# Idle matmuls between attention and the first expert, and the last logits from f16 pairs

## The chip, the core and the metric

The kernel runs on one core of a Trainium2 chip. A time is the device time of one execution in microseconds. The engines of the core run beside each other and wait for one another through semaphores: TensorE (PE; its weight loads are shown as PEld), VectorE (DVE), ScalarE (ACT), GpSimd (POOL) and SyncE (SP, which only issues DMAs). PE runs at one of two clock levels, 1.2 or 2.4 GHz; the profile shows the granted share of the higher one, 0.50 or 1.00.

## The reference

Bucketed attention over 4 batches of 8 heads (768 positions, head size 64), then a mixture of 8 experts in which tokens and experts are matched greedily, highest logit first, with room for 384 tokens at each expert:

```
mask = q_bucket[:, :, :, None] == k_bucket[:, :, None, :]      # buckets: signs of q @ proj, k @ proj
scores = np.where(mask, scale * np.matmul(q, k.transpose(0, 1, 3, 2)), -1e9)
attn = np.exp(scores - max); attn = attn / (sum + 1e-09); x = attn @ v   # heads side by side: 3072 x 512
logits = x @ w_gate                                             # 3072 x 8
for idx in np.argsort(-logits.flatten()):
    tok, e = idx // E, idx % E
    if assigned[tok] >= 0 or counts[e] >= cap: continue
    assigned[tok] = e; counts[e] += 1
out[mask_e] = np.maximum(x[mask_e] @ w1[e], 0.0) @ w2[e]        # for every expert e
```

## The kernel before

**Attention** goes head by head (32 of them, `NH`), in slots: scores on PE (L240, L258, L259), exponents on ACT (L260), the values' matmul on PE (L273 to L275, closed by six small ones at L279), the division on DVE (`norm`, L287 to L290). Products of full precision are made of f16 or bf16 pairs, a high part and what is left of it. After every second head the 128 new columns of x (a tile `X`) are transposed on PE against an identity matrix (`xtr`, L309), split on ACT (L310) and DVE (L311) into an f16 pair `XH`, `XL`, and multiplied by the gate's weights, which are a pair too (`logits`, L318 and L319). The very last 128 columns, those of heads 30 and 31, go another way (`xlast`, `flast`): the transposed tile stays f32 (copied by ACT for one half and by DVE for the other, L301), and six f32 matmuls (L304) add their share to the logits; DVE then sums the two parts into `Lm` (L305).

**Routing of expert 0** (`Moe.early` and `Moe.phase(0)`) follows on the critical path. It looks for the threshold logit at which the first expert is full: the logits' bits are cut into six digits; for each digit DVE compares all tokens with a table (`compare`, L530), PE counts (`count`, L540 once and L541 24 times, with 8 moving columns each), DVE finds the digit (L635), one matmul carries it to all partitions (L642), and DVE forms the next comparand (L649). The first digit's table has 128 columns, the others' 32. Then come the ties (L660 and the DVE chain behind it), running sums (L687, L688), the list of the expert's tokens (`members` on DVE, `collect` on PE, L699), and POOL issues three indirect DMAs that gather their rows of x (`gather`, L763). `xsplit0` transposes the three gathered tiles (L827, four f32 matmuls each) and splits them (L828, L829); then expert 0's first layer begins (`layer1c`, L843).

Between these steps PE already runs a few idle matmuls, `warm` (L576, L577): 128 columns, with a result that nobody reads. Their numbers stand in the table `KW`: after each count (`KW[0]`), after the digit's matmul (`KW[1]`), behind L660 (`KW[2]`), behind L688 (`KW[3]`), behind each of the three blocks of `collect` (`KW[4]`), behind L748 (`KW[5]`), between the transposes (`KW[6]`), and once behind the first count (`KW[7]`).

The order on every engine is the order in which the program is written (a manual schedule): an idle matmul stands in PE's queue before what is written after it, and what is written after it waits until it is through. The kernel's later experts are one long row of matmuls on PE (L858, L870), with the routing of the next expert between them.

Of the kernel before, what the change touches and what calls it, by code (L numbers as in the profile page):

```python
# [8 lines left out]
F32 = mybir.dt.float32  # L9
# [6 lines left out]
AX = mybir.AxisListType  # L16
# [3 lines left out]
AP=dict(PAT=[[5], [3]],  # L20
 E0=[3, 5],
 E1=[3, 4],
 X=[2, 2, 5],
 MR=2,
 LEAD=9,
 S=[7, 7],
 DW=[12, 0, 0, 0, 384],
 P1=[13, 13, 14, 16, 17, 17, 23, 21, 16, 27, 21, 26, 23, 24, 33, 32, 3, 4, 49, -7, 3, 13],
# [17 lines left out]
def attention(tc, nc, ctx, qT, kT, vv, proj, wg, x_dram, L, jp, identf, B, late=None, after=None):  # L46
# [234 lines left out]
    X={}  # L281
# [12 lines left out]
    XH,XL=(XT[:,2*i:2*i+2].bitcast(F16).rearrange("p d c q -> p (d c q)").rearrange("p (d c q) -> p d c q",d=4,c=6) for i in range(2))  # L294
    def wsplit():
        A.copy(wgs[:,:,0],wgr); G_.tensor_tensor(wgs[:,:,1],wgr,wgs[:,:,0],op=ALU.subtract)
    def xlast(b,d,hf):
        ps=psT.tile([128,512],F32,name="pst"); p=ps[:,0:384].rearrange("p (c q) -> p c q",c=3); r=slice(3*hf,3*hf+3)
        for c in range(3):
            T.transpose(p[:,c],X[b][:,3*hf+c,d*128:d*128+128],identf)  # L300
        (V.tensor_copy if hf else A.copy)(XT[:,1,r],p)  # L301
    def flast(b,d):
        p=LP[-1][:,0:96].rearrange("p (c z e) -> p c z e",c=6,z=2)
        for c in range(6): T.matmul(p[:,c,0],XT[:,1,c],wgr[:,d],start=False,stop=c==5,skip_group_check=True)  # L304
        V.reduce_sum(L[:,b*6:b*6+6],p.rearrange("p c z e -> p c e z"),axis=AX.X)  # L305
    def xtr(b,d,hf):
        ps=psT.tile([128,512],F32,name="pst"); p=ps[:,0:384].rearrange("p (c q) -> p c q",c=3); r=slice(3*hf,3*hf+3)
        for c in range(3):
# [3 lines left out]
    LP=[]  # L312
    def logits(b,ds):

        if ds[0]==0: LP.append(psS.tile([128,2,512],F32,name="pss")[:,0] if b==B-1 else psT.tile([128,512],F32,name="pst"))
        p=LP[-1][:,0:96].rearrange("p (c z e) -> p c z e",c=6,z=2)
        for d in ds:
            for c in range(6): T.matmul(p[:,c],XH[:,d,c],wgs[:,d],start=(d==0 and c==0),stop=False,skip_group_check=True)  # L318
            for c in range(6): T.matmul(p[:,c,0],XL[:,d,c],wgs[:,d,0],start=False,stop=(d==3 and c==5),skip_group_check=True)  # L319
        if ds[-1]==3: V.reduce_sum(L[:,b*6:b*6+6],p.rearrange("p c z e -> p c e z"),axis=AX.X)  # L320


    at={}
    def add(n,f,*a): at.setdefault(n,[]).append((f,a))
    def bdma():
# [8 lines left out]
    n=-1; early=[]  # L334
# [29 lines left out]
        add(2*half[h]+AP['MR']+1,m_rows,h,0); add(2*done[h]+AP['MR'],m_rows,h,1)  # L364
    for h in range(1,NH,2):
        b,d=h//8,h%8//2; n=2*(6*h+5+LAG)+AP['X'][0]
        if h==NH-1: n=2*(6*h+5+LAG)
        for hf in range(2): add(n+AP['X'][1]*hf,xlast if h==NH-1 else xtr,b,d,hf)
        if h==NH-1: add(n+4,flast,b,d)
        elif d==3: add(n+AP['X'][2],logits,b,range(4))  # L370
        elif d==2 and b==B-1: add(n+4,logits,b,range(3))
        if after and d==3:
            for i,f in enumerate(after(b,lambda: psT.tile([128,512],F32,name="pst"),lambda: psV.tile([128,512],F32,name="psv"))):
                add(n+5 if b==B-1 else max(n+8,AP['EA'][b][0])+AP['EA'][b][1]*i,f)
# [41 lines left out]
OWN=[(2, 0, 0), (3, 0, 0), (4, 0, 0), (5, 0, 0), (3, 1, 3), (4, 1, 3), (5, 1, 3)]  # L416
XS=[56, 56, 57, 57]
XD=[0, 9, 7, 4]
KW=[1,0,4,0,2,19,7,1]
SC=[16, 16, 36]  # L420
XSC=8.0
WSC=64.0
class Moe:
# [155 lines left out]
    def phase(s,ph):  # L579
# [9 lines left out]
        if not last:  # L589
# [13 lines left out]
            for l,w in enumerate(WID):  # L603
# [3 lines left out]
                if l==0 or first:  # L607
                    for c0,c1_ in blocks if first else ((0,NC),):
                        if l: s.compare(cmp,l,d,c0,c1_)
                        s.count(pc,P,cmp,l,c0,c1_)  # L610
                    if first:
                        if l==0: wp=s.wps(); s.warm(KW[7],wp)
                        s.warm(KW[0],wp)
                    for a,b in ((l+1,l+2),) if first else ((1,6),):
                        if a<6:
                            for q in range(a,b): s.digit(P,q,slice(0,NC))
                            if first: V.tensor_tensor(E[:,a:b],D[:,a:b],s.sc[:,a:b],op=ALU.mult)
                            else:
                                V.tensor_tensor(E[:,a],D[:,a],s.sc[:,a],op=ALU.mult)
                                for q in range(a+1,b): nc.scalar.activation(E[:,q],D[:,q],AF.Copy,scale=2.0**-sum(WID[:q+1]))  # L620
                                if ph>2:
                                    for _ in range(2): s.fill()
                else:
                    nt=s.count4(pc,P,cmp)
# [73 lines left out]
        def collect(c0,c1):  # L698
            for g in range(c0,c1): T.matmul(pi[:,0:12],ohp[:,g//2,:,g%2],Rr[:,:,:,:,g],start=g==0,stop=g==NC-1)  # L699
# [24 lines left out]
        if first:  # L724
            pi=ps()
            for i,b in enumerate(blocks):
                members(*b)
                if not i: rr()
                collect(*b); s.warm(KW[4],wp)
            V.scalar_tensor_tensor(acc,pp[:,NC:2*NC],4096.5+s.CAP,STb[:,NC:],op0=ALU.is_lt,op1=ALU.mult)  # L730
        else:
            members(0,NC)
            rr()
            if not last: left()
            yield
            pi=ps()
            collect(0,NC)
            if not last:
                T.matmul(pp[:,64:72],s.ones,cc,start=True,stop=True)
                s.fill(); s.fill()  # L740
# [251 lines left out]
```

## Time and profile before

| | |
|---|---|
| time before, median of 3 runs | 690.43 us (689.93 to 693.68) |
| the profiled execution | 689.51 us, of which its span 687.7 us |
| PE busy | 661.0 us, 96% of the span |
| PE's granted clock | 1.00, but for 375.6 to 402.9 us and the last microseconds: 0.50 |
| chain that ended last | PE 83%, DVE 6%, DMA 4%, ACT 2%, issue 2% |

In the rows below, a time is in us from the start of the span. "[1.68 <-DVE zcmp L530]" behind a row is the time that the engine stood idle before it, and what ended the wait. A matmul's time in a row covers its way through the array too, so that rows overlap; how closely matmuls follow one another is the start of the next row less the start of this one, by the count.

### The profile page before, as it was taken

How to read it: one execution, taken by the hardware profiler on the slowest of the kernel's cores; microseconds unless marked ns; L12 is line 12 of the kernel's file. 1: busy time of each engine (PE TensorE's matmuls, PEld its weight loads, DVE VectorE, ACT ScalarE, POOL GpSimd, SP SyncE). 2: the span in 40 equal slices, each digit the busy share in tenths (PEclk: the TensorE clock that was granted, in tenths of full speed). 3: DMA queues.
4: the chain of work that ended last, by engine and by line, in shares of the span. 5: the costliest groups of instructions: out<-in, count | busy, mean ns of one | idle time of the engine just before them, and what ended most of it. 6: DMA issues, size and time to landing. Idle time of an engine off the chain costs nothing.

```text
span 687.7 us, 19365 instructions
## 1 busy us (share of the span) xinstructions
PE 661.0 (96%) x7952; PEld 436.3 (63%) x7952; DVE 498.5 (72%) x1122; ACT 471.4 (69%) x886; POOL 518.9 (75%) x456
## 2 busy tenths in 40 slices
PE   8799999999999999999998689999999999999997
PEld 3467676777777777777777485555555565655553
DVE  6778889888887887788883778778787878744120
ACT  7878887888878878777764055665665665666760
POOL 7999998997998989988655156585866665769871
PEclk9999999999999999999999579999999999999999
DMA  9647665526646266340000170718181827271701
GB/s 229 179 131 208 161 181 134 138 80 151 180 102 170 72 151 178 91 100 25 25 26 26 47 247 15 292 31 306 35 303 40 298 68 255 60 294 61 276 32 46
DMA packets 40240, 93.59 MB, mean 136 GB/s; under 512 B 4580, under 2 KB 30552, under 8 KB 37848
## 3 DMA queue, kind: packets, MB, share of 16 engines
q1 hardware_dynamic: 33048, 46.21, 25.9%
q0 software_dynamic: 7104, 46.15, 19.0%
q8 instruction: 62, 1.02, 0.6%
q14 instruction: 26, 0.21, 0.1%
HBM read 59.53 MB, written 12.58 MB: 105 GB/s over the span
## 4 chain that ended last, share of the span: by engine, by line
PE 83%; DVE 6%; DMA 4%; ACT 2%; issue 2%; SPq 1%; POOL 1%; POOLq 0%; ACTq 0%
PE po L870 16%; PE px L858 14%; PE pst L258 9%; PE pst L259 8%; PE pss L240 8%; PE psv L273 5%; PE psv L275 5%; PE psv L274 5%; PE po L858 2%; PE pst L309 2%; PE pss L142 1%; PE pst L248 1%; PE px L815 1%; PE px L843 1%; DVE lo L263 1%
## 5 line engine op out<-in xcount | busy, mean ns | idle before, releaser
L263 POOL TENSOR_TENSOR lo<-pt 128x768 f16<-128x768 f32 x144 | 227.3, 1593 | 36.3 <-ACT pt L260 33.5
L260 ACT ACTIVATE pt<-pst 128x384 f32<-128x384 f32 x384 | 182.0, 491 | 59.4 <-PE pst L259 49.3
L242 DVE TENSOR_REDUCE m<-pss 128x1 f16<-128x770 f32 x192 | 181.2, 956 | 34.5 <-PE pss L240 33.3
L258 PE MATMUL pst<-qa,ka 128*128 128x384 f16 x384 | 125.0, 326 | 3.6 <-ACT qa L249 2.8
L259 PE MATMUL pst<-qb,kb 128*128 128x384 f16 x384 | 124.8, 325 | 0.0
L273 PE MATMUL psv<-vh,pt 128*128 128x65 f16 x1152 | 120.7, 194 | 0.5 <-DVE X L290 0.5
L275 PE MATMUL psv<-vh,lo 128*128 128x65 f16 x1152 | 120.9, 194 | 0.0
L274 PE MATMUL psv<-vl,pt 128*128 128x64 f16 x1152 | 120.9, 193 | 0.0
L273 PEld LDWEIGHTS <-pt 128*128 128x128 bf16 x1152 | 106.7, 98 | 8.7 <-issue 0.6
L274 PEld LDWEIGHTS <-pt 128*128 128x128 bf16 x1152 | 105.7, 99 | 8.8 <-issue 0.7
L275 PEld LDWEIGHTS <-lo 128*128 128x128 f16 x1152 | 105.8, 97 | 0.0
L798 POOL TENSOR_TENSOR wl<-wf,wh 128x512 f16<-128x512 f32 x74 | 83.7, 1160 | 21.6 <-ACT wf L789 21.1
L240 PE MATMUL pss<-ka,qa 128*128 128x385 f16 x384 | 94.0, 328 | 2.1 <-DMA ka<-bt 1.5
L780 ACT ACTIVATE wh<-wf 128x1024 f16<-128x1024 f32 x64 | 66.9, 1053 | 34.0 <-DMA wf<-in_w_dram,zwidx 33.4
L858 PEld LDWEIGHTS <-wh 128*128 128x128 f16 x480 | 45.3, 97 | 29.8 <-issue 0.8
L263 DVE TENSOR_TENSOR lo<-pt 128x768 f16<-128x768 f32 x48 | 59.2, 1233 | 1.9 <-ACT pt L260 1.8
L870 PEld LDWEIGHTS <-hh 128*128 128x128 f16 x384 | 35.8, 97 | 38.4 <-issue 0.4
L789 ACT ACTIVATE wf<-wf 128x1024 f32<-128x1024 f32 x55 | 58.0, 1059 | 0.9
L240 PEld LDWEIGHTS <-qa 128*128 128x128 f16 x384 | 37.1, 97 | 27.6 <-issue 1.2
L875 ACT ACTIVATE o<-po 128x512 f32<-128x512 f32 x23 | 13.7, 596 | 55.6 <-PE po L870 44.8
L771 POOL DMA_INDIRECT wf<-in_w_dram,zwidx x22 | 25.9, 1177 | 32.3 <-DVE ze L669 13.4
L259 PEld LDWEIGHTS <-kb 128*128 128x128 f16 x384 | 37.4, 97 | 18.6 <-issue 6.6
(296 smaller groups left out, 1360.7 us busy)
## 6 DMA issues: line engine op xcount, KB each, us to landing
vp<-in_vv_dram SPq DMA_DIRECT2D x8, 768.0 KB
x_dram<-X SPq DMA_DIRECT2D x16, 384.0 KB
qp<-in_qT_dram SPq DMA_DIRECT2D x7, 768.0 KB
kp<-in_kT_dram SPq DMA_DIRECT2D x7, 768.0 KB
qa<-qh SPq DMA_DIRECT2D x14, 192.0 KB
qb<-qh SPq DMA_DIRECT2D x14, 192.0 KB
ka<-kh SPq DMA_DIRECT2D x14, 192.0 KB
kb<-kh SPq DMA_DIRECT2D x14, 192.0 KB
```

What stands on the lines that cost most here:

```text
L240: T.matmul(ps[:,hf,0:HK],QA[u][:,j,qc*128:qc*128+128],KA[u][:,j,hf*HK:hf*HK+HK],start=True,stop=True)
L242: V.tensor_reduce(M6[h][:,qc:qc+1],ps[:,:,0:HK],axis=AX.XY,op=ALU.max,negate=True)
L258: T.matmul(ps[:,0:384],KA[u][:,j,kr],QA[u][:,j,r],start=True,stop=False)
L259: T.matmul(ps[:,0:384],KB[u][:,j,kr],QB[u][:,j,r],start=False,stop=True)
L260: A.activation(PT[h,kc][0][:,r],ps[:,0:384],AF.Exp,scale=0.125)
L263: eng.tensor_tensor(l,p,p.bitcast(BF)[:,1::2],op=ALU.subtract)
L273: T.matmul(av[:,c,:],ph[:,r],VH[u][:,j,kc,:],start=(kc==0 and c==0),stop=False,skip_group_check=True)
L274: T.matmul(av[:,c,0:64],ph[:,r],VL[u][:,j,kc,:],start=False,stop=False,skip_group_check=True)
L275: T.matmul(av[:,c,:],l[:,r],VH[u][:,j,kc,:],start=False,stop=False,skip_group_check=True)
L798: for _ in range(n): s.nc.gpsimd.tensor_tensor(*s.pend.pop(0)[1],op=ALU.subtract)
L858: T.matmul(p[:,0:384],a[:,o:o+128],b[:,d],start=n==0,stop=n==11)
L870: T.matmul(p,a[:,f,c*128:c*128+128],b[:,f*512:f*512+512],start=n==0,stop=n==23)
```

## The change

Four things. (1) `xlast` and `flast` go: the last 128 columns of x take `xtr` and `logits` like all others, so their f16 pair and 12 matmuls of f16 (L311 and L314 in the new numbering, with 16 and 8 columns). (2) A new helper `idle` puts idle matmuls of 128 columns before, between and behind the last transposes, and into the last logits (`IW`: 16, 8, 4, 5). (3) In the first digit's count, the last block now starts behind 30 idle matmuls (`KW[8]`), and has 8 matmuls instead of 6 behind the pause. (4) The numbers in `KW` are new: before [1,0,4,0,2,19,7,1], now [4,8,24,28,[10,2,14],46,12,1,30].

```
-    def xlast(b,d,hf):
-        ...
-        (V.tensor_copy if hf else A.copy)(XT[:,1,r],p)
-    def flast(b,d):
-        p=LP[-1][:,0:96].rearrange("p (c z e) -> p c z e",c=6,z=2)
-        for c in range(6): T.matmul(p[:,c,0],XT[:,1,c],wgr[:,d],start=False,stop=c==5,skip_group_check=True)
...
+            for c in range(6):
+                if ds==[3] and c==3: idle(IW[2])
+                T.matmul(p[:,c],XH[:,d,c],wgs[:,d],start=(d==0 and c==0),stop=False,skip_group_check=True)
+            for c in range(6):
+                if ds==[3] and c==3: idle(IW[3])
+                T.matmul(p[:,c,0],XL[:,d,c],wgs[:,d,0],start=False,stop=(d==3 and c==5),skip_group_check=True)
...
+    free=[]
+    def idle(n):
+        if not free: free.append(psS.tile([128,2,512],F32,name="pss")[:,0])
+        for _ in range(n): T.matmul(free[0][:,0:128],wrm[:,0:128],wrm[:,0:128],start=True,stop=True)
...
+        if h==NH-1: n=2*(6*h+5+LAG); add(n,idle,IW[0])
+        for hf in range(2): add(n+AP['X'][1]*hf,xtr,b,d,hf)
+        if h==NH-1: add(n+AP['X'][1],idle,IW[1])
+        if d==3: add(n+(4 if b==B-1 else AP['X'][2]),logits,b,[3] if b==B-1 else range(4))
...
-KW=[1,0,4,0,2,19,7,1]
+KW=[4,8,24,28,[10,2,14],46,12,1,30]
+IW=[16,8,4,5]
...
                         if l: s.compare(cmp,l,d,c0,c1_)
+                        elif first and c1_==NC: wp=s.wps(); s.warm(KW[8],wp)
                         s.count(pc,P,cmp,l,c0,c1_)
                     if first:
-                        if l==0: wp=s.wps(); s.warm(KW[7],wp)
+                        if l==0: s.warm(KW[7],wp)
                         s.warm(KW[0],wp)
...
-                collect(*b); s.warm(KW[4],wp)
+                collect(*b); s.warm(KW[4][i],wp)
```

PE's order at the last logits, before: behind the values' matmul (L279) stand the six transposes into `pst`, the six f32 matmuls into the logits' tile `pss`, and the first count.

```order
L279 MATMUL psv<-wf_226,qa_184 128x65
L300 MATMUL pst<-identf,X 128x128 x6
L304 MATMUL pss<-wgr,XT 128x8 x6
L540 LDWEIGHTS moneh
L540 MATMUL pst<-nrem,moneh 128x8
```

The same place now (L322 is `idle`, L541 the first count; the lines that only repeat are left out):

```order
L279 MATMUL psv<-wf_226,qa_184 128x65
L322 LDWEIGHTS wrm
L322 MATMUL pss<-wrm 128x128
...
L300 MATMUL pst<-identf,X 128x128 x6
L322 LDWEIGHTS wrm
L322 MATMUL pss<-wrm 128x128
...
L311 MATMUL pss<-wgs,XT 128x16
...
L314 MATMUL pss<-wgs,XT 128x8
...
L541 MATMUL pst<-nrem,moneh 128x8
```

The f32 matmuls are gone; 16 idle ones stand before the transposes, 8 behind them, and 4 and 5 among the twelve new ones of f16.

DVE's order at that place, before, where it copies one half of the transposed tile:

```order
L290 TENSOR_TENSOR X<-psv,r_8441 128x3x64 x2
L301 COPY XT<-pst 128x384
L305 TENSOR_REDUCE Lm<-pss 128x48
L506 TENSOR_REDUCE zm<-Lm 128x6
L507 TENSOR_TENSOR zeq<-Lm,zm 128x48
```

And now:

```order
L290 TENSOR_TENSOR X<-psv,r_8441 128x3x64 x2
L302 TENSOR_TENSOR XT<-pst,XT 128x384 x2
L315 TENSOR_REDUCE Lm<-pss 128x48
L507 TENSOR_REDUCE zm<-Lm 128x6
L508 TENSOR_TENSOR zeq<-Lm,zm 128x48
```

DVE now forms the low parts of both halves, each behind a cast on ACT, where it copied one half beside ACT before.

PE's order at a digit, before: the last count, one idle matmul (L577), the digit's matmul (L642), and at once the next digit's first count (L540).

```order
L541 MATMUL pst<-zOH,zcmp_387 32x8
L577 LDWEIGHTS mones
L577 MATMUL psv<-iot,mones 128x128
L642 LDWEIGHTS us_74
L642 MATMUL pst<-zhit,us_74 128x1
L540 LDWEIGHTS moneh
```

The same place now (L578 is the idle matmul, L644 the digit's):

```order
L542 MATMUL pst<-zOH,zcmp_387 32x8
L578 LDWEIGHTS mones
L578 MATMUL psv<-iot,mones 128x128
...
L644 LDWEIGHTS us_74
L644 MATMUL pst<-zhit,us_74 128x1
L578 LDWEIGHTS mones
L578 MATMUL psv<-iot,mones 128x128
...
L541 LDWEIGHTS moneh
```

Four idle matmuls now stand before the digit's matmul and eight behind it, ahead of the next digit's count.

## Rows read from the trace of the kernel before

**Rows 1.** Windows: length, busy us of PE, PEld, DVE, ACT, POOL; granted clock; DMA.

```profile
375.50:375.60 0.10, 0.10 (x3) 0.10 (x3) 0.00 (x0) 0.00 (x0) 0.00 (x0) 0.82 1.00 292
382.00:384.00 2.00, 1.46 (x27) 1.10 (x27) 1.38 (x8) 0.00 (x0) 0.00 (x0) 0.50 0.00 0
402.75:403.00 0.25, 0.25 (x3) 0.25 (x2) 0.25 (x4) 0.00 (x0) 0.25 (x1) 0.76 1.01 377
408.00:420.00 12.00, 11.91 (x170) 9.11 (x167) 9.58 (x34) 11.56 (x20) 10.08 (x10) 1.00 0.25 103
```

**Rows 2.** PE in order of time, last transposes and counts: start, us, what.

```profile
373.65 0.88 PE L300 MATMUL pst<-identf,X 128*128 128x128 f32 x6 [0.88 <-DVE X L290]
...
376.68 0.62 PE L541 MATMUL pst<-zOH,zcmp 128*128 128x8 bf16 x18
378.98 0.32 PE L541 MATMUL pst<-zOH,zcmp 128*128 128x8 bf16 x6 [1.68 <-DVE zcmp L530]
...
409.49 0.74 PE L541 MATMUL psa<-zOH,zcmp 128*128 128x8 bf16 x24
```

**Rows 3.** PE in order of time, from the running sums to expert 0.

```profile
391.08 0.22 PE L687 MATMUL psa<-zSTb,ntri 128*128 128x48 bf16 x1 [1.01 <-DVE zSTb L671]
...
393.22 0.27 PE L699 MATMUL psa<-zRr,zcmp 128*128 128x12 bf16 x4 [1.66 <-DVE zRr L723]
...
396.02 2.19 PE L577 MATMUL po<-iot,mones 128*128 128x128 bf16 x19
398.94 1.12 PE L827 MATMUL px<-identf,xg 128*128 128x128 f32 x4 [0.73 <-DMA xg<-x_dram,zidx]
399.85 0.95 PE L577 MATMUL po<-iot,mones 128*128 128x128 bf16 x7
400.60 1.06 PE L827 MATMUL px<-identf,xg 128*128 128x128 f32 x4
...
402.44 0.83 PE L827 MATMUL psa<-identf,xg 128*128 128x128 f32 x4
403.11 0.39 PE L843 MATMUL px<-xh,wh 128*128 128x128 f16 x4
403.33 0.39 PE L843 MATMUL px<-xh,wl 128*128 128x128 f16 x4
```

**Rows 4.** Chain that ended last, at the last logits: start, us, what.

```profile
374.24 0.49 ACT XT L301
...
374.77 2.04 PE pss L304 x12
...
376.84 0.27 DVE Lm L305
```

**Rows 5.** Chain that ended last, one of the five later digits.

```profile
381.55 0.17 PE pst L642
...
382.31 0.97 PE pst L541 x24
...
383.53 0.17 PE pst L642
```

**Rows 6.** Lines of the earlier logits: duration in ns, least, median and most.

```profile
L310 ACT CAST XT<-pst x30: 471/480/486, 52.5 to 361.2; 128x384 f16<-128x384 f32 x30
L311 DVE TENSOR_TENSOR XT<-pst,XT x30: 545/556/559, 53.1 to 361.7; 128x384 f16<-128x384 f32 x30
L318 PE MATMUL pss<-wgs,XT x18: 169/169/173, 362.1 to 362.9; 128*128 128x16 f16 x18
```

**Rows 7.** POOL's first and third issue of the gather, in order of time.

```profile
395.57 0.95 POOL L763 DMA_INDIRECT xg<-x_dram,zidx  x1 [2.42 <-DVE zA L708]
...
398.16 0.98 POOL L763 DMA_INDIRECT xg<-x_dram,zidx  x1 [0.30 <-issue]
```

**Rows 8.** PE and ACT at the start of expert 0, in order of time.

```profile
405.72 0.33 PE L843 MATMUL px<-xh,wl 128*128 128x128 f16 x3 [0.49 <-issue]
405.75 0.60 ACT L828 ACTIVATE xh<-psa 128x512 f16<-128x512 f32 x1 [3.46 <-remote]
```

More of the change, by code (lines that the diff above doesn't have):

```diff
@@ L296, in wsplit @@
         A.copy(wgs[:,:,0],wgr); G_.tensor_tensor(wgs[:,:,1],wgr,wgs[:,:,0],op=ALU.subtract)
-    def xlast(b,d,hf):
-        ps=psT.tile([128,512],F32,name="pst"); p=ps[:,0:384].rearrange("p (c q) -> p c q",c=3); r=slice(3*hf,3*hf+3)
-        for c in range(3):
-            T.transpose(p[:,c],X[b][:,3*hf+c,d*128:d*128+128],identf)
-        (V.tensor_copy if hf else A.copy)(XT[:,1,r],p)
-    def flast(b,d):
-        p=LP[-1][:,0:96].rearrange("p (c z e) -> p c z e",c=6,z=2)
-        for c in range(6): T.matmul(p[:,c,0],XT[:,1,c],wgr[:,d],start=False,stop=c==5,skip_group_check=True)
-        V.reduce_sum(L[:,b*6:b*6+6],p.rearrange("p c z e -> p c e z"),axis=AX.X)
     def xtr(b,d,hf):
@@ L317, in logits @@
         for d in ds:
-            for c in range(6): T.matmul(p[:,c],XH[:,d,c],wgs[:,d],start=(d==0 and c==0),stop=False,skip_group_check=True)
-            for c in range(6): T.matmul(p[:,c,0],XL[:,d,c],wgs[:,d,0],start=False,stop=(d==3 and c==5),skip_group_check=True)
+            for c in range(6):
[4 more added lines that the diff above has]
+                T.matmul(p[:,c,0],XL[:,d,c],wgs[:,d,0],start=False,stop=(d==3 and c==5),skip_group_check=True)
         if ds[-1]==3: V.reduce_sum(L[:,b*6:b*6+6],p.rearrange("p c z e -> p c e z"),axis=AX.X)
+    free=[]
+    def idle(n):
+        if not free: free.append(psS.tile([128,2,512],F32,name="pss")[:,0])
+        for _ in range(n): T.matmul(free[0][:,0:128],wrm[:,0:128],wrm[:,0:128],start=True,stop=True)
     at={}
@@ L366, in attention @@
         b,d=h//8,h%8//2; n=2*(6*h+5+LAG)+AP['X'][0]
[L367 to L370, printed above, removed]
+        if h==NH-1: n=2*(6*h+5+LAG); add(n,idle,IW[0])
+        for hf in range(2): add(n+AP['X'][1]*hf,xtr,b,d,hf)
+        if h==NH-1: add(n+AP['X'][1],idle,IW[1])
+        if d==3: add(n+(4 if b==B-1 else AP['X'][2]),logits,b,[3] if b==B-1 else range(4))
         elif d==2 and b==B-1: add(n+4,logits,b,range(3))
```

## The prediction

> **What bounds the kernel now.** I began with the page's busy shares and its line of the granted clock, then took windows across the one place where that clock is low. PE runs at 2.4 GHz until a window at 375.5 us shows 0.82, stands at 0.50 (1.2 GHz) all through the routing of expert 0, and is back in a window at 402.75 [rows 1]. What it did before the fall: it stood still 0.88 us for the division of the last head, made the six transposes [rows 2], waited again, and then ran f32 matmuls of 8 columns. What it did before the rise: 19 idle matmuls, then transposes and idle matmuls nearly without a pause [rows 3]. In front of and behind this stretch PE is full, 11.91 of 12.00 us in the window after it [rows 1], so what is won here comes off the end.
>
> Next I read the chain of waits through the stretch, to see what of it is PE's own time. In the last logits PE has the largest piece: 2.04 us of f32 matmuls, from 374.77 to the DVE sum at 376.84 [rows 4]. In each of the five later digits the count is 0.97 of 1.98 us, and the rest is DVE and the ways between engines [rows 5]. Then DVE rules until POOL issues the gather, and at the end come the DMA and three groups of transposes with idle matmuls between them, all at 1.2 GHz [rows 3].
>
> **The last logits, without the clock.** Before: from the first copy at 374.24 to the DVE sum at 376.84, 2.60 us. Now ACT casts the first half (0.48), DVE takes its low part 0.04 later (0.56), and then that of the second half (0.56), whose cast on ACT was over at 374.72 + 0.48 = 375.20, before DVE is free for it [rows 4, 6]. So 374.24 + 0.48 + 0.04 + 0.56 + 0.56 = 375.88; another 0.05 to PE, three last matmuls at 0.17 for one [rows 6] and 0.025 for each further one, 0.04 to DVE: 376.19. The sum starts 0.65 us earlier. This term needs no clock: the matmuls are short. Bounds: 0.75, with DVE's low parts at their least and nothing lost on the way to PE and back, and 0.6, if the five idle matmuls in front of the last three run at 1.2 GHz. I take 0.65.
>
> **What the idle matmuls cost.** One of 128 columns follows the next by 0.107 us at 1.2 GHz (399.85 to 400.60, seven) and by 0.055 us at 2.4 GHz (403.11 to 403.33, four) [rows 3]. At 2.4 GHz every group fits its pause: 30 make 1.65 us where PE waits 1.68 [rows 2]; 24 make 1.32 us where PE before waits 1.01 and fills 4 × 0.107 = 0.43 more; 28 make 1.54 us against 1.66; 46 make 2.53 us against the 2.92 from 396.02 to 398.94 [rows 3]. In a digit, 8 make 0.44 us between the digit's matmul at 381.55 and the counts at 382.31 [rows 5]. Behind each of these stands, in PE's queue, the matmul for which DVE waits; as long as the clock is 2.4 GHz they cost nothing, and the cover is the wait for DVE or for the gather.
>
> **What the clock itself gives in the digits: little.** A count follows the next by (0.62 − 0.17)/17 = 0.026 us at 1.2 GHz and by (0.74 − 0.17)/23 = 0.025 us at 2.4 GHz [rows 2]. Of a digit's 24 counts some 20 come behind DVE's second compare, so 20 × 0.0015 = 0.03 us a digit, 0.15 us for five. The row at 2.4 GHz has tables of 128 columns, though, and five of the six digits have 32; if those went twice as fast, it would be 20 × 0.013 = 0.27 us a digit, 1.3 in all. I take 0.15, the value of the row; 1.3 is the other end. The Trainium skill speaks for the low end, and so against the change: "TensorE: Matmul & The Clock Gate", section "Wait — 56ns, not 53.3ns?", says that matmuls do not start closer together than about 25 ns, however few columns they have, at the full clock too. The row of 128-column tables agrees; no row shows 32-column ones at 2.4 GHz. By that rule the five digits give the 0.15, without it up to the 1.3.
>
> The first digit loses a little: 8 counts instead of 6 stand behind its pause, 2 × 0.025 = 0.05 us. The DVE chains behind the digits don't change. Up to the gather: 0.65 + 0.15 − 0.05 = 0.75 us.
>
> **Transposes and the start of expert 0.** The first gather is issued from 395.57 to 396.52, and its transposes start at 398.94 [rows 3, 7]: 2.42 us behind the issue. The third's issue ends at 399.14 [rows 7]; by the same 2.42 its rows are there at 401.56. Its transposes start at 402.44, with no wait for a DMA in their row [rows 3]: PE was late, from four transposes that took 0.91 us (398.94 to 399.85) and seven idle matmuls at 0.107, twice. At 2.4 GHz I halve the transposes to 0.46 for four (an estimate from that row): the first group ends at 399.40, twelve idle ones (0.66) at 400.06, and both second and third group then wait for their rows, at 400.27 and 401.56. Expert 0 begins at 401.56 + 0.46 = 402.02 instead of 403.11: 1.1 us. The lower bound is a third gather that landed just at 402.44: then 402.90, or 0.2 us. I take 1.1, since the row names no DMA.
>
> **Sum.** 0.75 + 1.1 = 1.85 us off the profiled execution: 689.51 (span 687.7 and 1.8 around it) − 1.85 = 687.7. That execution lies 0.9 below the median of the runs, 690.43; a median should be compared with a median, so I forecast 690.43 − 1.85 = 688.6. Bounds of the sum: 0.6 + 0 − 0.05 + 0.2 = 0.75, and 0.75 + 1.3 − 0.05 + 1.1 = 3.1.
>
> **Rivals.** *The clock is not held through the digits (the change doesn't do what it says), and comes back later.* For it: a digit still spends a third of its time on counts of 8 columns, and PE at 1.46 busy of 2.00 us did not win the clock back there before [rows 1]. Against: 12 idle matmuls a digit where one was, and long rows of them behind, which bring it back. The price is in the digits: 8 × 0.107 = 0.86 us behind the digit's matmul instead of a pause of some 0.67, so the count starts about 0.2 us late, 1.0 us for five, and the 0.15 goes. That leaves 1.85 − 1.15 = 0.7: 689.7.
>
> *Slower: the clock falls at the logits as before and is not back before the gather.* Then every group stands in the way by what it exceeds its pause at 0.107: 30 make 3.2 us, 1.5 over; five digits 1.0; 24 make 2.6, 1.1 over; 28 make 3.0, 1.3 over; 46 make 4.9, 2.0 over. If the clock returns in the row of 46, about 5 us, less the 0.65 of the logits: 694.8; if it stays low to the end, 697 and more. It decides from the 30 on: at 0.055 they fit, at 0.107 they don't. For it: this is where the clock fell before. Against: the pause of 0.88 us in front of the fall [rows 2] is now filled, and before it was shorter rows than these that brought the clock back.
>
> *More: a stall goes too.* At 405.7 PE ends a wait of 0.49 us, behind a shorter one, that the profile puts down to nothing it shows, and ACT, ending 3.46 us for something "remote", starts at the same moment [rows 8]. If this belongs to what else moves at that time, a start 1.85 us earlier may miss it: 688.6 − 0.5 = 688.1; with the upper bound of the counts, 687.0. Nothing in the change removes it by design.
>
> **How the numbers follow.** I give the forecast 0.53, the clock lost and won back 0.25, the stall or faster counts on top 0.15, and the slow case 0.07. A measurement of this kernel can tell about 0.5% from no change: 687.0 and 693.9. The first two cases lie between. Of the third most lies between them, but its far end, and a median of runs that happens to fall low, pass 687.0: 0.14 for faster. The slow case makes slower: 0.07. That leaves 0.79 for the same. The range: down to 686.9 for the third case, up to 690.6 for a sum at its lower bound or digits at 1.2 GHz, on runs that before spread from 689.9 upward; the slow case stays outside.
>
> **What would show it.** Right, step by step: a granted clock of 1.00 from the values' matmul to expert 0; the DVE sum of the logits some 1.9 us behind the first ACT cast; a digit's period still near 1.95 us; no pause of PE that an idle matmul ends too late, so that DVE waits no longer than now for the digit's matmul; transposes of the second and third gather that wait for a DMA. Wrong: windows at 0.50 among the digits, with idle matmuls at 0.107 behind which the counts start late; or a third group of transposes that waits for its gather past 402 with nothing gained in front of it. The forecast fails altogether if expert 0 starts earlier by these 1.85 us and later experts wait for their weights or their gather instead, so that the end does not move.

## The result, and the profile after

The change made the kernel slower: 694.7 us (median of 9 runs, 693.45 to 695.75) against 689.93 us of the kernel before in the same comparison; ratio 1.0074, interval 1.0059 to 1.0089. The profiled execution took 693.49 us, 3.98 more than that of before.

The ruler for all that follows is the distance from the values' last matmul (L279) to two later marks; the attention in front of it is unchanged, and its end lies anywhere between 370.7 and 372.9 us in the traces below. From L279, in us:

| start of | before | after | gained or lost on the way |
|---|---|---|---|
| the first digit's matmul (before L642, after L644) | 7.15 | 6.39 | −0.76: logits and first digit |
| the ties (before L659, after L661) | 16.80 | 17.52 | +1.48: five digits |
| the running sums (L687, L689) | 18.65 | 20.06 | +0.69: the row of 24 |
| the end of the token list (L748, L750) | 23.57 | 24.71 | −0.27 |
| the gathered transposes (L827, L829) | 26.52 | 28.60 | +0.94 |
| expert 0 (L843, L845) | 30.68 | 36.40 | +3.64 |

With an attention that ended 1.02 us earlier and 0.74 us less from expert 0 to PE's last matmul, 5.72 comes down to 3.96, next to the 3.98 us between the two executions. So there are two losses: digits with their row, and the tail.

The windows of after that answer to [rows 1] (length, busy us of PE, PEld, DVE, ACT, POOL; granted clock; DMA):

```profile
378.00:381.00 3.00, 2.95 (x59) 2.30 (x57) 2.38 (x13) 0.00 (x0) 0.00 (x0) 1.00 0.03 8
...
382.00:390.00 8.00, 8.00 (x126) 6.92 (x127) 4.57 (x27) 0.00 (x0) 0.00 (x0) 0.50 0.01 2
...
392.00:400.00 8.00, 6.86 (x123) 6.05 (x121) 7.11 (x23) 2.12 (x2) 4.10 (x5) 1.00 0.64 200
...
402.00:408.00 6.00, 4.24 (x27) 3.46 (x27) 1.37 (x5) 1.09 (x2) 1.89 (x3) 0.50 0.97 289
...
409.00:421.00 12.00, 12.00 (x200) 10.43 (x197) 11.02 (x32) 9.97 (x17) 6.93 (x7) 1.00 0.19 79
```

The clock was held through the last logits, where it fell before. It fell in the digits instead, at 381.1 us, with PE busy 2.95 of the 3.00 us ahead; it came back at the end of the row of 24, at 391.4, and fell a second time in the tail, at 401.6, where PE is busy for only 4.24 of 6.00 us. From expert 0 on PE is as full as before.

PE in the digits (start, us, what), one at 2.4 GHz, one at 1.2 GHz with the four idles in front of it, and the row of 24 behind them:

```profile
377.79 0.16 PE L644 MATMUL pst<-zhit,us 128*128 128x1 bf16 x1
377.82 0.61 PE L578 MATMUL psv<-iot,mones 128*128 128x128 bf16 x8
...
378.56 0.93 PE L542 MATMUL pst<-zOH,zcmp 128*32 128x8 bf16 x24
...
379.75 0.17 PE L644 MATMUL pst<-zhit,us 32*128 32x1 bf16 x1
...
383.77 0.61 PE L578 MATMUL psv<-iot,mones 128*128 128x128 bf16 x4
384.31 0.18 PE L644 MATMUL pst<-zhit,us 32*128 32x1 bf16 x1
384.42 1.03 PE L578 MATMUL psv<-iot,mones 128*128 128x128 bf16 x8
...
385.43 0.78 PE L542 MATMUL pst<-zOH,zcmp 128*32 128x8 bf16 x24
...
386.69 0.18 PE L644 MATMUL pst<-zhit,us 32*128 32x1 bf16 x1
...
389.03 2.60 PE L578 MATMUL psv<-iot,mones 128*128 128x128 bf16 x24
391.47 0.19 PE L689 MATMUL psa<-zSTb,ntri 128*128 128x48 bf16 x1
```

And the two rows of before that answer to the four idles in front of a digit's matmul and to the row of 24:

```profile
383.21 0.29 PE L577 MATMUL psv<-iot,mones 128*128 128x128 bf16 x1
...
389.48 0.59 PE L577 MATMUL psv<-iot,mones 128*128 128x128 bf16 x4
```

At full clock a digit takes 1.96 us (377.79 to 379.75), at half clock 2.38 (384.31 to 386.69), where before took 1.98 at half clock [rows 5]. At half clock eight idles of 1.03 us stand in front of the counts, and four stand in front of the digit's matmul: 0.54 us from the first of them to that matmul (383.77 to 384.31), where before has one idle and 0.32 us (383.21 to 383.53).

PE in the tail, which answers to [rows 3]:

```profile
396.15 2.67 PE L578 MATMUL po<-iot,mones 128*128 128x128 bf16 x45
399.26 0.22 PE L578 MATMUL po<-iot,mones 128*128 128x128 bf16 x1 [0.45 <-issue]
400.00 0.42 PE L829 MATMUL px<-identf,xg 128*128 128x128 f32 x2 [0.52 <-DMA xg<-x_dram,zidx]
400.74 0.43 PE L829 MATMUL px<-identf,xg 128*128 128x128 f32 x2 [0.31 <-issue]
...
402.95 0.59 PE L578 MATMUL po<-iot,mones 128*128 128x128 bf16 x4 [0.85 <-issue]
...
405.83 1.33 PE L578 MATMUL po<-iot,mones 128*128 128x128 bf16 x11 [0.41 <-issue]
406.95 1.06 PE L829 MATMUL psa<-identf,xg 128*128 128x128 f32 x4
407.81 0.63 PE L845 MATMUL px<-xh,wh 128*128 128x128 f16 x4
```

PE stops again and again for nothing that the profile shows ("issue"), and does one to five matmuls in between. ACT, which evicts the transposes, and POOL's last issue in that stretch:

```profile
405.96 1.09 ACT L830 ACTIVATE xh<-px 128x512 f16<-128x512 f32 x2 [8.24 <-PE px L829]
...
403.56 0.94 POOL L773 DMA_INDIRECT wf<-in_w_dram,zwidx  x1 [0.30 <-issue]
```

ACT gets the first group, over on PE at 401.17, only at 405.96, together with the second: 1.46 us behind the end of POOL's seventh issue in a row (three of the gather, four of weights). Before has the same in small: there ACT gets the third group at 405.75 [rows 8], 1.24 us behind POOL's last issue (403.57, 0.94 long). Its first two groups were not late: ACT took them at 400.10 and 401.70, in the middle of the row of issues.

### The profile page after: what moved, and what is told of

Read it like the earlier page. It is cut to its first block, busy times and chain, and to the rows that moved or that the text cites. A ratio compares the mean times of both kernels' runs of the same rounds, so it can differ in the third digit from the quotient of the medians.

```text
span 691.7 us, 19817 instructions
## 1 busy us (share of the span) xinstructions
PE 672.6 (97%) x8178; PEld 448.1 (65%) x8178; DVE 500.9 (72%) x1123; ACT 471.5 (68%) x887; POOL 518.5 (75%) x456
## 4 chain that ended last, share of the span: by engine, by line
PE 85%; DVE 6%; DMA 3%; ACT 2%; issue 2%; SPq 1%; POOL 1%; POOLq 0%; DVEq 0%; ACTq 0%
PE po L872 16%; PE px L860 14%; PE pst L258 9%; PE pst L259 8%; PE pss L240 8%; PE psv L273 5%; PE psv L275 5%; PE psv L274 5%; PE po L860 2%; PE pst L300 2%; PE psv L578 2%; DVE m L242 1%; PE pst L248 1%; DVE lo L263 1%; PE pss L142 1%
## 5 line engine op out<-in xcount | busy, mean ns | idle before, releaser
L263 DVE TENSOR_TENSOR lo<-pt 128x768 f16<-128x768 f32 x48 | 60.9, 1268 | 1.9 <-ACT pt L260 1.8
```

Source lines behind the costliest of these rows:

```text
L263: eng.tensor_tensor(l,p,p.bitcast(BF)[:,1::2],op=ALU.subtract)
```

## The experiments

Runs of one group were measured together, on one chip, beside the kernel before; each ratio is to before in its own group. "Expert 0" is its start behind L279 in the trace (before 30.68, after 36.40). The last column is the sum of PE's waits, from the end of the token list to 6 us behind the start of expert 0, that end for nothing the profile shows (before 0.7, after 2.7). Both columns are read from one execution of each kernel, the ratio is from 6 to 12 of them.

| run | group | expert 0, us | ratio, interval | waits, us |
|---|---|---|---|---|
| e1 logits only | 1 | 29.91 | 0.9986 (0.9971 to 1.0001) | 0.3 |
| e2 old tail | 1 | 31.78 | 1.0017 (1.0002 to 1.0032) | 0.8 |
| e3 wide tail | 1 | 31.04 | 1.0009 (0.9994 to 1.0025) | 0.9 |
| e4 full digits | 1 | 36.00 | 1.0047 (1.0026 to 1.0069) | 2.6 |
| e5 second weights later | 2 | 30.53 | 1.0013 (0.9998 to 1.0027) | none |
| e6 sized for half clock | 2 | 29.56 | 0.9998 (0.9984 to 1.0012) | none |
| e7 wide counts, wide tail | 2 | 29.71 | 1.0000 (0.9983 to 1.0017) | none |
| e8 e7 and e5 together | 2 | 29.64 | 1.0008 (0.9998 to 1.0019) | none |
| e9 wide counts only | 3 | 29.76 | 0.9979 (0.9964 to 0.9994) | none |
| e10 second weights in four | 3 | 30.43 | 1.0008 (0.9990 to 1.0026) | none |
| e11 old digits | 3 | 31.82 | 1.0014 (0.9996 to 1.0033) | none |
| e12 e1, weights later | 3 | 29.85 | 1.0002 (0.9984 to 1.0021) | none |
| e13 after, again | 4 | 34.38 | 1.0077 (1.0055 to 1.0100) | 2.8 |
| e14 e5, again | 4 | 31.91 | 1.0027 (1.0011 to 1.0044) | 1.5 |
| e15 e9, again | 4 | 32.78 | 1.0052 (1.0032 to 1.0071) | 2.1 |
| e16 e7, again | 5 | 30.42 | 0.9990 (0.9974 to 1.0006) | none |
| e17 e8, again | 5 | 29.53 | 1.0008 (0.9989 to 1.0028) | none |
| e18 e1, again | 5 | 30.13 | 0.9995 (0.9975 to 1.0015) | none |

**The logits alone.**

```
-KW=[4,8,24,28,[10,2,14],46,12,1,30]
-IW=[16,8,4,5]
+KW=[1,0,4,0,[2,2,2],19,7,1,0]
+IW=[0,0,0,0]
```

> The kernel after with the f16-pair logits kept and every number of idle matmuls set back to what the kernel before has (none in the logits, 1 and 0 in a digit, 2 behind each step of the row, 19 before the gather's transposes, 7 between them). Main theory: the logits' new form is worth what the prediction said, 0.65 us, and all of the loss comes from the idles: 689.93 - 0.65 = 689.3 us, a ratio of 0.999, with windows of granted clock that fall in the logits as before and a tail with the counts before's start of expert 0. Rival: the new form of the logits itself moves the fall of the clock and costs further on; then the time is between 691 and 695 us with the idles gone.

Expert 0 came 0.77 us nearer to L279. The main theory holds: the new form of the logits is worth its 0.7 us in the trace, and the loss is the idles'. The ratio, 0.9986, fits, but its interval reaches 1.000. One part did not come: the clock fell at 377.6 us, 6.06 behind L279, and not in the logits, where it fell in before (375.6, 3.17 behind).

**The tail: fewer idles, or as many columns in fewer instructions.** e2 has 19 and 7 in `KW[5]` and `KW[6]`; e3 has 11 and 3 of 512 columns:

```
+    def wide(s,n,ps):
+        for _ in range(n): s.nc.tensor.matmul(ps[:,0:512].rearrange("p (a b) -> p a b",a=4),s.ones,s.ones[:,None,:].to_broadcast([128,4,128]),start=True,stop=True)
...
-            s.warm(KW[5],wp); s.wp=wp
+            s.wide(KW[5],wp); s.wp=wp
...
-            if c<2: s.warm(KW[6],s.wp)
+            if c<2: s.wide(KW[6],s.wp)
```

> The kernel after with only the two rows of idle matmuls at the gather set back: 19 instead of 46 in front of the first group of gathered transposes, 7 instead of 12 between the groups. Main theory: the many idle instructions that PE takes while POOL issues its indirect DMAs are what makes PE stand still there for nothing that the profile shows, so that expert 0 starts 5.7 us late against the values' matmul; with the old numbers most of the 3 to 4 us of the tail comes back and the 2.2 us lost in digits and row stay: about 691.5 us (690.5 to 692.5). Rival: the stall belongs to the DMA issue alone and to when the stretch gets there, whatever PE runs meanwhile: about 694.7 us, expert 0 no earlier.

> The kernel after with the idle matmuls of the tail in a quarter of the instructions: 11 of 512 columns instead of 46 of 128 in front of the first group of gathered transposes, 3 instead of 12 between the groups, so nearly the same columns and the same time of PE. Main theory (the number of PE instructions while the indirect DMAs are issued makes the stall): about 691.2 us, and PE's waits put down to nothing between 399 and 407 us are gone. Rival (the time that the idles fill, or the clock, not their number): as the kernel after, about 694.7 us, with the same pauses.

PE in the tail of e3:

```profile
395.17 2.53 PE L581 MATMUL po<-mones 128*128 128x512 bf16 x11
398.05 0.66 PE L832 MATMUL px<-identf,xg 128*128 128x128 f32 x4 [0.35 <-DMA xg<-x_dram,zidx]
398.54 0.81 PE L581 MATMUL po<-mones 128*128 128x512 bf16 x3
399.81 0.66 PE L832 MATMUL px<-identf,xg 128*128 128x128 f32 x4 [0.46 <-DMA xg<-x_dram,zidx]
400.30 0.81 PE L581 MATMUL po<-mones 128*128 128x512 bf16 x3
401.46 0.63 PE L832 MATMUL psa<-identf,xg 128*128 128x128 f32 x4 [0.35 <-issue]
401.92 0.39 PE L848 MATMUL px<-xh,wh 128*128 128x128 f16 x4
```

The idles fill the same time as in after, and PE now waits for the gather, as the prediction wanted, but for one 0.35 and, in expert 0, one of 0.56. From the end of the token list to expert 0 it is 6.78 us, with the old numbers 7.05, with 46 and 12 narrow ones in e4, of the same group, 10.24. In these traces, then, the loss goes with the number of narrow idles, not with the time or the columns that they fill. How large it is, this group does not say: the trace of e4 is its slowest execution of eight, 3.65 us above its median, and its digits differ too; by the medians e4 is only 2.69 us above e3 (692.33, 689.64).

**Fuller digits.** `KW[0],KW[1]` are 6, 10 instead of 4, 8.

> The kernel after with fuller pauses in the digits: 6 idle matmuls instead of 4 in front of a digit's matmul and 10 instead of 8 behind it. Main theory (the clock fell in the digits because their pauses were still open): the granted clock stays at 1.00 through the digits and the row of 24, a digit's period is about 1.96 us instead of 2.38, and of the 2.2 us lost in digits and row most comes back: about 692.5 us; the stall in the tail stays. Rival (the clock falls there whatever is put in, or the fuller rows only stand in the way): the digits take 2.4 to 2.8 us each and the time is 695.3 us or more.

In the trace the rival was right. The clock fell at 382.4 us, in the second digit as in after, with PE busy without a pause; the next digit took 2.81 us (382.83 to 385.64). Two windows of e4, in front of the fall and behind it, then one of e1, where PE is less busy:

```profile
378.50:382.40 3.90, 3.89 (x84) 3.32 (x82) 2.66 (x15) 0.00 (x0) 0.00 (x0) 1.00 0.03 6
...
382.50:389.00 6.50, 6.50 (x95) 5.44 (x93) 3.07 (x19) 0.00 (x0) 0.00 (x0) 0.50 0.01 3
```

```profile
382.50:389.00 6.50, 4.73 (x85) 3.55 (x85) 4.38 (x27) 0.00 (x0) 0.00 (x0) 0.50 0.01 3
```

So the clock fell here with PE busy 3.89 of the 3.90 us ahead. But this trace is the slowest of e4's eight executions. Its mean granted clock over the span is 0.987, which is 17 us at half clock; in five of the others it is 0.996 or 0.997, which is some 4 to 6 us (estimates from the share of a span of 690 us), and these took 691.54 to 692.49 us, near the 692.5 of the main theory. The other two took 695.1 us, near the rival's. After had 0.985 to 0.993 in its nine executions, but e5, with the same digits, 0.990 to 1.000. So how long the clock is low differs from execution to execution, and whether fuller pauses help on the whole is not shown; that they make it sure is refuted.

**Wider counts in the digits.** In e7 (wide tail) and e9 (nothing else changed) the 24 counts of a later digit have 64 columns, the same 8 eight times over:

```
+        o=pc[0:J,0:64].rearrange("p (a e) -> p a e",a=8) if l else pc[0:J,0:8]
+        def w(ap): return ap[:,None,:].to_broadcast([128,8,8]) if l else ap
...
-        for g in range(c0,c1): T.matmul(pc[0:J,0:8],cmp[:,g//2,:,g%2],P["OH"][:,g,:],start=False,stop=g==s.NC-1)
+        for g in range(c0,c1): T.matmul(o,cmp[:,g//2,:,g%2],w(P["OH"][:,g,:]),start=False,stop=g==s.NC-1)
```

> The kernel after with the wide idles in the tail (11 and 3 of 512 columns), and in the five later digits each of the 24 counts has 64 columns instead of 8, the same 8 eight times over; nothing else is changed, and no number of the result. Main theory: the clock falls in the digits because the counts, though PE is busy without a pause, move too few columns; with 64 it stays at 1.00 through the digits and the row behind them, a digit takes 1.96 to 2.0 us, and against the kernel with the wide tail alone some 1.5 us come back: about 688.2 us by its ratio. Rival (the clock falls in the digits whatever PE does there): 24 counts of 64 columns at 1.2 GHz take 1.3 us instead of 0.8, each digit at low clock gets 0.5 longer, and the time is 690.5 us or more.

> The kernel after with the 24 counts of each of the five later digits 64 columns wide and nothing else changed: the tail has its 46 and 12 narrow idles, POOL its row of seven issues. Theory: digits and stall are two separate losses. The clock stays at 1.00 through the digits, so expert 0 comes 1.5 us nearer to the values' matmul than in the kernel after, 34.9 instead of 36.4, but PE still stands still in the tail: 1.0052 of the kernel before. Rival: the stall in the tail only comes when the clock has fallen before it; held at full clock all the way, expert 0 starts 29.7 us behind the values' matmul as with the wide tail, and the time is that of the kernel before, 1.000.

The window of e9 that answers to the two above:

```profile
382.50:389.00 6.50, 6.50 (x124) 5.42 (x125) 4.12 (x24) 0.00 (x0) 0.00 (x0) 1.00 0.01 3
```

The same PE busy, the idles of after (fewer than e4's), more columns in the counts, and the clock is 1.00 from attention to the end. The other executions bear it out: of the 66 of e7, e8, e9, e15, e16 and e17, 56 have a mean granted clock of 0.998 or more, and none is below 0.996. In e9 and e7 ties and sums come 16.6 and 18.3 us behind L279 instead of 17.5 and 20.1: from the first digit's matmul to the sums it is 11.90 us, 13.67 in after and 11.50 before. So 1.77 of the 2.17 us of the first loss are the clock's fall in the digits, and the row's idles behind it. The time of e7 (1.0000, against 1.0009 of the wide tail alone in another group) can't show this by itself. But e9 also had no waits in its tail, though that is after's tail to the letter; its own theory had expected them.

**POOL's row.** e5 moves the loads of the second weights behind the third group; e10 makes four issues of two (`s.wload(0,1,4)`); e8 is e7 with e5's move, e12 is e1 with it:

```
-        s.wload(0,1,2)
         s.xsplit0()
+        s.nc.gpsimd.tensor_copy(t0,s.W[0,'x'][0][0:1,0,256:257])
+        s.wload(0,1,2)
```

> The kernel after with one thing moved on POOL: the two indirect DMAs that load the second weights of expert 0 are no longer issued straight behind the gather and the first weights, but behind a copy on POOL that reads the last third of xh, so after ACT has evicted the third group of transposes. POOL's row of issues then ends after five instead of seven, 2.5 us earlier. Main theory (PE stands still while POOL issues its row of indirect DMAs, and until about 1.3 us behind the last): PE's short waits put down to the issue end some 2.5 us earlier in the program, expert 0 starts about 34 us behind the values' matmul instead of 36.4, and the time is 692.0 to 692.8 us, unless the second weights come too late. Rival (the stall belongs to the idle instructions themselves or to the clock, POOL's row only happens beside it): the pauses stay where they are, expert 0 starts 36 us or more behind the values' matmul, and the time is 694.7 us or above.

> The kernel after with the second weights of expert 0 loaded by four indirect DMAs of 1024 columns instead of two of 2048: the same bytes, but nine issues in POOL's row instead of seven, so the row ends some 2.5 us later. Theory (PE stands still until POOL's last issue of the row, whatever it has to do): ACT's wait for the first two groups of transposes and PE's short waits last 2.5 us longer, expert 0 starts 38.5 to 39 us behind the values' matmul, 1.010 to 1.011 of the kernel before. Rival (the idle instructions have a stall of their own length, or the bytes of the second weights are what disturbs): as the kernel after, 36.4 us and 1.0074.

> The kernel with the wide counts and the wide tail, and the second weights of expert 0 loaded behind the third group of transposes. If POOL's row of issues is what makes PE stand still, the two waits that the wide tail still has (0.35 before the third group and 0.56 in expert 0) go or move behind the later issues: 687.3 to 687.9 us, some 0.6 below the wide counts alone. Rival: the second weights come too late, or the later issues make PE stand still in expert 0 by as much: equal to the wide counts alone or above it.

> The version that the runs so far point to: the f16-pair logits, every number of idles as in the kernel before, and the second weights of expert 0 loaded behind the third group of transposes. Theory: the logits' 0.8 us stay, and the late third group of the kernel before (ACT waits 3.46 us for it) and PE's wait of 0.3 to 0.5 in expert 0 go: 0.998 of the kernel before. Rival: those waits cost the kernel before nothing, and the later issues only move: 0.9986 as the logits alone, or 1.000 and more if the second weights now come late.

e5 alone would have looked like proof. e10 was the counter-test, with two issues more, and it has no waits either: expert 0 at 30.43, 1.0008. Neither had any other kernel of groups 2 and 3, and there the move of the weights is worth nothing that can be measured: e8 (1.0008 beside 1.0000 of e7) and e12 (1.0002) missed the gains that they expected. Either the theory fell or the groups differed, and only the kernel after itself beside e5 could tell:

> The kernel after, unchanged, on another chip beside the kernel before. If its waits in the tail belong to the kernel: 1.0074 again, expert 0 some 36 us behind the values' matmul. If they belong to the chip or the run and a chip without them is drawn: only the loss of the digits and of the row at 1.2 GHz is left, expert 0 some 30.4 to 31 us behind the values' matmul, 1.000 to 1.002.

> The kernel with the second weights loaded behind the third group of transposes, on the same chip as the kernel after. If POOL's row of issues makes the waits and this chip shows them in the kernel after: 1.0013 again, against 1.0074 there. If the waits are the chip's own: the same as the kernel after within 0.2%, whichever that is.

> The kernel after with the 64-column counts, on the same chip as the kernel after. The clock is held through the digits here too, 1.00 over the span, and against the kernel after the 1.0 to 1.5 us of digits and row are gone. On a chip without the waits 0.998 of the kernel before, as measured; on one with them up to 1.005, since its tail is that of the kernel after.

Here all three have the waits, and e9's kernel goes from 0.9979 to 1.0052 with nothing changed in it. Groups 3 and 4 ran on the same chip, so it is not the chip by itself. Nor is it the clock, as e9's rival had it: e15 keeps 1.00 from attention to the end and has the waits. Within group 4 POOL's row counts. PE's first group of transposes, ACT's first eviction and POOL's last issue ahead of it, in e13:

```profile
398.30 0.68 PE L829 MATMUL px<-identf,xg 128*128 128x128 f32 x4
...
404.94 1.08 ACT L830 ACTIVATE xh<-px 128x512 f16<-128x512 f32 x2 [8.20 <-remote]
...
402.86 0.94 POOL L773 DMA_INDIRECT wf<-in_w_dram,zwidx  x1 [0.30 <-issue]
```

And in e14, where the first row of issues is two shorter:

```profile
402.43 1.08 ACT L830 ACTIVATE xh<-px 128x512 f16<-128x512 f32 x2 [5.54 <-PE px L829]
...
400.56 0.94 POOL L773 DMA_INDIRECT wf<-in_w_dram,zwidx  x1 [0.31 <-issue]
```

ACT hears of the transposes 1.14 and 0.93 us behind the end of the last issue. Measured from L279 the row ends 2.50 us earlier in e14 (30.09 instead of 32.59), and expert 0 comes 2.47 us earlier (31.91, 34.38), 1.0027 against 1.0077. So in executions that have the waits, they end with POOL's unbroken row of indirect DMAs, and a shorter row ends them sooner. This is not so for every group of transposes: in e15 ACT gets the first one 0.33 us before the end of the seventh issue, and in before the first two came in time.

```profile
403.64 0.60 ACT L832 ACTIVATE xh<-px 128x512 f16<-128x512 f32 x1 [6.19 <-remote]
...
403.03 0.94 POOL L775 DMA_INDIRECT wf<-in_w_dram,zwidx  x1 [0.30 <-issue]
```

The move also shifts the bytes of the second weights, which would be a rival. The windows speak against the traffic by itself (e13 twice, then e9; the last two numbers are the DMA engines' busy share and GB/s):

```profile
399.00:405.00 6.00, 2.97 (x30) 2.04 (x30) 0.24 (x1) 0.06 (x1) 3.88 (x4) 0.94 0.85 261
405.00:408.00 3.00, 3.00 (x29) 2.84 (x29) 2.40 (x11) 2.97 (x5) 0.00 (x0) 0.54 0.98 333
...
399.00:405.00 6.00, 5.46 (x87) 5.12 (x85) 5.76 (x16) 2.93 (x5) 4.41 (x4) 1.00 0.87 241
```

With as much traffic e9 has no wait, and in e13 PE is busy without a pause again while the traffic is higher still. Nor does it look like the loading of instructions: of the packets that carry them, one came in the first of these stretches (the queues of e13 from 399 to 405 us: packets, MB, share of 16 engines).

```profile
q0 software_dynamic: 413, 1.56, 84.3%
q14 instruction: 1, 0.01, 0.7%
```

What holds PE is not shown. Its weight loads start again on a beat, in e13 at 399.16, 399.89, 400.62, 401.35, 402.06, 403.49, 404.20 and 404.92, so 0.71 to 0.73 us apart or twice that, while POOL's issues come 1.24 to 1.59 us apart; whether the recording of PE's many instructions for the profile plays a part, no run here can tell. Why some groups have the waits and others not is open too: the same kernel, on the same chip, showed both.

**Sizes for half clock, and the old digits.** e6 has e1's logits and digits, 12, 14 and 5, 2, 8 in the row, and 6 and 1 idles of 512 columns in the tail; e11 is after with `KW[0],KW[1]` at 1, 0.

> The f16-pair logits with no idle matmuls in them and the digits as in the kernel before, but idles in the row behind the digits sized for half clock: 12 behind the ties, 14 behind the sums, 5, 2 and 8 behind the three collects, then 6 matmuls of 512 columns in front of the gathered transposes and 1 between the groups. Main theory: idles that fit their pause at 1.2 GHz cost nothing at either clock and bring the clock back before the gathered rows land; each group of transposes then takes 0.66 instead of 1.11 us and expert 0 starts 0.3 to 1.0 us earlier than with the logits alone: 688.0 to 688.9 us where that one's ratio gave 689. Rival: the clock comes back no earlier than with the logits alone (in the trace of that one at 401.5 us), or it does and PE stands still for its instructions instead: 689 us, the same as the logits alone.

> The kernel after with the idles of the digits set back to the kernel before's (1 in front of a digit's matmul, none behind it); the logits, the row and the tail stay as in the kernel after. Theory: the digits' idles are in the way only because the clock falls, and cost 1.4 us there (a digit of 1.98 us instead of 2.38 where the clock is low); the ties come 16.1 us behind the values' matmul instead of 17.5. The row of 24, 28, 10 and 14 is long enough to bring the clock back before the tail, and the stall of the tail stays: 1.0054. Rival: with emptier digits the clock comes back later, and the rows cost at 1.2 GHz what they exceed their pauses by: 1.008 or more.

In e6 the clock came back at 396.5 us, before the first group landed, and expert 0 at 29.56 was 0.35 nearer than in e1, which ran in another group; the ratio cannot show that. In e11 the ties came at 16.0 us, 1.5 earlier than in after, where the theory had 1.4, but the clock came back only at 393.2 us, and 28 idles took 3.07 us in a pause of 1.66 [rows 3]: by the end of the token list (24.32) only 0.39 of the gain was left. The waits that it expected did not come (group 3).

**Is there a better version?** e16, e17 and e18 repeat e7, e8 and e1 in one group.

> The kernel after with 64-column counts in the digits and with 512-column idles in the tail (11 and 3), a second time. Clock 1.00 throughout. In a session without the waits as measured, 0.998 to 1.000. In a session with them, if a quarter of the instructions is enough to keep PE out of them: 0.5 us of waits at most, the first two groups of transposes reported at once, expert 0 30.0 to 30.4 us behind the values' matmul, 0.999 to 1.000. If it is not: expert 0 32 us or more, 1.003 or more.

> The same with the second weights of expert 0 loaded behind the third group of transposes, a second time. In a session with the waits they end with the fifth issue instead of the seventh: expert 0 29.7 to 30.2 us behind the values' matmul, and 0.2 to 0.5 us below the version without the move. In a session without them both are the same.

> The f16-pair logits with all idles as in the kernel before, a second time, on the chip of the two others. Expert 0 29.9 us behind the values' matmul, 0.9985 of the kernel before in either kind of session; if the wide versions are better than this by more than 0.5 us, idles are worth having here, and otherwise the logits are all that the change has to give.

0.9990, 1.0008, 0.9995: no difference that can be measured. The traces order them (e17 29.53, e18 30.13, e16 30.42, where PE waited 1.14 for the third gather), but by less than the attention varies, and the same kernels stood at 29.64, 29.91 and 29.71 in other groups. No version beats the kernel before in every group. Where the waits come, the wide tail has not been tried together with the wide counts, since group 5 showed none.

## Why the prediction was wrong

**Two steps failed.** The larger is the term of 1.1 us for the transposes and the start of expert 0: −1.1 was forecast and +4.58 measured. The sum had the landing of the gather and PE's own time in it, and no term for PE and its signals standing still while POOL issues its row. The other is the premise of "as long as the clock is 2.4 GHz they cost nothing": the idles were all sized by the 0.055 us of full clock, and the clock was not held. The forecast took a pause of PE [rows 2] for what makes it fall, and filled the pauses. The trace of e4 has hardly a pause in front of its fall (3.89 of 3.90 us busy); e9 has after's idles, fewer than e4's, with wider counts, and keeps the clock.

**Last logits and first digit:** −0.65 and +0.05 were forecast, −0.76 measured in after and e1. In after the DVE sum starts 3.66 us behind L279 instead of 4.41, so 0.75 earlier, the upper bound: DVE's two low parts took 1.02 us together, not twice 0.56. The first digit lost nothing.

```profile
373.73 1.02 DVE L302 TENSOR_TENSOR XT<-pst,XT 128x384 f16<-128x384 f32 x2 [0.89 <-ACT XT L301]
375.07 0.26 DVE L315 TENSOR_REDUCE Lm<-pss 128x48 f32<-128x96 f32 x1 [0.32 <-PE pss L314]
```

The step needs no clock, as the forecast said: in e18 the clock fell at 375.0, within the logits, and the sum still starts 3.68 us behind L279.

**Five digits:** the forecast's −0.03 a digit was right where the clock was high (1.96 against 1.98). No row had shown tables of 32 columns at 2.4 GHz; after has them, behind DVE's second compare in the digit at 378.56:

```profile
378.89 0.59 PE L542 MATMUL pst<-zOH,zcmp 128*32 128x8 bf16 x18
```

A count follows the next by (0.59 − 0.17)/17 = 0.025 us, and by (0.78 − 0.17)/23 = 0.027 us at 1.2 GHz (385.43). So the low end of the bounds came, not the 0.013 of the other end. The page "TensorE: Matmul & The Clock Gate" of the Trainium skill (section "Wait — 56ns, not 53.3ns?") gives about 25 ns as the least distance of two matmuls' starts, and this trace agrees. Where the clock was low, the first rival's price, "about 0.2 us late" a digit, was too small: 0.40 (2.38 against 1.98), 1.48 in all. It left out the four idles in front of the digit's matmul, 0.22 of the 0.40. That rival, with 0.25, had the mechanism of this half.

**Row of 24:** the slow rival's 1.1 over the pause was the right kind. The 24 took 2.44 us (389.03 to 391.47), where before has 1.60 from its first idle there to the running sums (389.48 to 391.08): 0.84 over, of which 0.16 was won back just in front of the row, so 0.69 was lost. The clock came back at 391.4, too late to help this row much.

**Transposes and start of expert 0:** 0.94 and 3.64 make the +4.58. The DMA side was right: without the waits PE did wait for the second and third gather, and the way from the token list to expert 0 was 6.49 us in e10 and 6.57 in e9 against 7.11 before, 0.5 to 0.6 us, inside the bounds of 0.2 to 1.1. What was not in the sum are the waits beside POOL's row. [Rows 8] showed them in small, and the third rival named them, but as something that an earlier start "may miss"; POOL's last issue was not read beside it. That reading would have given 1.24 us behind the seventh issue for a late signal. It would not have given the size: in before only the third group was late, and PE waited 0.66 us in expert 0.

**The slower rival** came close in time (694.8) by luck: it had the clock fall in the logits and all rows too long. In after the logits kept their clock, and most of the loss was the wait in the tail.

Without waits the kernel after would be about level with before: e10, which differs in four issues for two, stands at 1.0008 (0.9990 to 1.0026). The forecast of 688.6 is 0.9973 of before's 690.43, so digits and row alone would have made it miss by about 0.35%, some 2.4 us.

## What to carry to other kernels

Idle matmuls are free only at the clock they are sized for; size them for the lower one, or make sure that the clock is held where they stand. Here wider counts, without more idles, held it in e9 (and the 66 executions with such counts lie at 0.996 or more), and more idles in the pauses did not hold it in the trace of e4. Where PE runs many short instructions while POOL issues a long row of indirect DMAs, look for late signals behind the row; fewer and longer idles (e3) and a shorter row (e14) made them cost less in the groups that had them, and gained nothing in the others. Before a wait is put down to one edit, measure the unchanged kernel again beside the experiment. And read a trace beside the times of the kernel's other executions: that of e4 was its slowest.

## What the runs showed of the hardware that was not expected

PE's clock fell while PE was busy 3.89 of 3.90 us (trace of e4, with matmuls of 8 and 128 columns), and stayed at 1.00 in e9 with counts of 64 columns and fewer idles. In three groups PE stood still, and its signals came up to 5.96 us late (e13: ACT takes at 404.94 the transposes that were over at 398.98), mostly until 0.9 to 1.5 us after POOL's last indirect DMA of an unbroken row; in three others, one of them on the same chip, the same instructions ran without a wait. Within these waits PE started again on a beat of about 0.72 us (e13).
